# An attention, mixer and expert kernel on one core: the order of all steps read from a table instead of planned, and a third output tile

## The chip, the core and the metric

The kernel runs on one core of one Trainium2 chip. The metric is device microseconds of one execution; less is better. A core has a matrix engine (TensorE, PE in the profile; its weight loads are listed apart as PEld), VectorE (DVE), ScalarE (ACT), GpSimd (POOL), and queues that issue transfers; nearly all of this kernel's transfers are issued by SyncE (SP). Every engine takes its instructions strictly in the order in which the program lists them, and semaphores make one engine wait for another. So an instruction that has to wait holds up everything that stands behind it on its engine.

## The reference

Three layers are computed one after the other for B = 4 sequences of S = 448 tokens with 768 features.

```python
# 1: attention, 12 heads of 64, q and k normalized by their root mean square
q_n, k_n = rmsnorm(q, g_q), rmsnorm(k, g_k)
x = softmax(q_n @ k_n.T / 8) @ v                    # heads side by side: (4, 448, 768)
# 2: mixer: over tokens (448 -> 256 -> 448), then over channels (768 -> 1536 -> 768)
u = x + (relu(x.T @ w_tok1) @ w_tok2).T
x = u + relu(u @ w_ch1) @ w_ch2
# 3: four causal attention "experts" of width 64; each token takes the best two by a gate
logits = x @ w_gate
for e in range(4):
    ye = causal_softmax(x @ wq[e], x @ wk[e]) @ (x @ wv[e]) @ wo[e]
    out += gate(logits, e) * ye
```

All inputs and the output are float32.

## The kernel before

**Stages.** The work is cut by sequence b (0 to 3). For each b there are six pairs of heads of the first attention (`Pair`: `load`, `stack`, `score`, `finish`), the token mixer (`token`), the channel mixer (`channel`), the projections and gate of the experts (`project`), two causal pairs and the output product (`combine`). Pairs are numbered through in tile names, by their keys: k0 to k5 belong to the first sequence, k6 to k11 to the second, k12 and k13 are the first sequence's causal pairs, k14 to k19 belong to the third sequence, and so on. The softmax of one sequence's attention runs beside the channel mixer of the sequence before it, which is nearly pure matrix work.

**Products.** `product` makes a 32-bit product out of three matmuls per block, on operands that were split into a high and a low half (`mm3`, L526; tiles a<-uhl,whl or a<-hid,whl in the profile). `split` makes the two halves: a copy (L437 on ACT, L438 on DVE) and a subtraction (L456, DVE or POOL). The channel weights are split once, stored, and loaded again for later sequences (whl<-kept_c).

**Softmax of a pair.** `weighted` multiplies q by k in row halves of the array (L608), takes the row maxima on DVE (L578), multiplies them by the factors of q's norm (`scale`, L584, DVE or POOL), and takes exponentials on ACT (L593). The weights are then transposed: on the matrix engine for the first nine pairs (`flip`, L632; L656 in causal pairs) or, later, in 32x32 blocks on DVE (`turn`: L706, then sixteen copies per pair, L718, on ACT, DVE or POOL). `attend` multiplies by v in column halves of the array (L731). For the norms, squares are taken on ACT (L876, L886) or POOL (L887) and summed on DVE (L834), and a short chain takes the inverse root (`root`, L843 to L852); from b = 0, pair 2 on, the factors of k are stored to memory (rs<-st, L906), read back spread over partitions (rb<-rs, L971) and multiplied into k (`scaled`: one DVE instruction at L826, or two of POOL at L828 and L829). The channel mixer adds its result into u at L1115 on DVE, the output product leaves through an `ot` tile (L437 or L438) and a store (L1205).

**What sets the order.** No order is written out. `add` records each step with the engines that may do it, an assumed cost on each, what it reads and writes, and how PE's array is split (`mode`: rows, columns or whole). Ring sizes (`RING`) say how many tiles of a name exist; a step that opens a tile waits until the users of the tile that had the place are done. `order` then lays all steps out ten times by priorities (`lay`), with assumed lags between engines (`LAG`), an assumed cost for a change of the array's split (`TURN`) and a clock model, keeps the shortest plan, and `issue` emits the steps in that order, each on the engine that the plan chose.

## Time and profile before

| | us |
|---|---|
| median of 3 runs | 865.03 (862.51 to 867.0) |
| the profiled execution, its own time | 864.52 |
| its span, first to last instruction | 862.6 |
| outside the span | 1.9 |
| PE busy | 818.5 |
| DVE busy | 621.6 |
| ACT busy | 465.4 |
| POOL busy | 159.1 |

The durations below belong to the profiled execution. PE is busy in 95% of the span, but ends of matmuls are modelled, so busy time also holds short waits. The mean granted TensorE clock is 0.994 of full speed.

### The profile page before, as it was taken

The numbers are of one execution on the slowest core, as the hardware profiler recorded it, in microseconds if no ns is written. First come the engines' busy times: TensorE is split into PE (matmuls) and PEld (weight loads), VectorE is DVE, ScalarE is ACT, GpSimd is POOL, SyncE is SP. The second block draws the span as 40 slices with busy tenths as digits, with TensorE's granted clock in tenths as the row PEclk, the third lists the DMA queues.
The fourth block names the chain that finished last, engine by engine and source line by source line (L and its number), as shares of the span: only waits on it lengthen the run. The fifth ranks groups of instructions, "written<-read, shape, count | busy, mean of one in ns | idle before, by whom it ended". The sixth has DMA issues, their size and how long they took to land.

```text
span 862.6 us, 13161 instructions
## 1 busy us (share of the span) xinstructions
PE 818.5 (95%) x4508; PEld 634.1 (74%) x4508; DVE 621.6 (72%) x1290; ACT 465.4 (54%) x1046; POOL 159.1 (18%) x173
## 2 busy tenths in 40 slices
PE   3888889999989999999999998999999999999998
PEld 1445578877765877887676786897776799998787
DVE  6988889999999878826989777933888781114352
ACT  6897765757798546504676554700757631011443
POOL 1243831110463222002132111110130100000000
PEclk9999989999999999999999999999999999999999
DMA  8555678999788927887655514786464406666344
GB/s 235 170 156 150 186 231 267 297 300 298 253 290 229 266 96 224 251 245 212 199 158 157 176 58 135 219 244 214 146 189 132 129 31 217 207 231 203 106 132 168
DMA packets 83202, 168.37 MB, mean 195 GB/s; under 512 B 17504, under 2 KB 39136, under 8 KB 83136
## 3 DMA queue, kind: packets, MB, share of 16 engines
q1 hardware_dynamic: 82992, 167.54, 63.7%
q8 instruction: 36, 0.59, 0.3%
q14 instruction: 30, 0.25, 0.1%
q10 hardware_dynamic: 144, 0.00, 0.0%
HBM read 136.66 MB, written 30.84 MB: 194 GB/s over the span
## 4 chain that ended last, share of the span: by engine, by line
PE 67%; DVE 15%; ACT 6%; DMA 6%; issue 3%; POOL 2%; SPq 1%; ACTq 0%; DVEq 0%; POOLq 0%
PE a L526 49%; PE m L731 8%; PE s L608 7%; ACT s L593 3%; DVE nm L578 3%; DMA w<-in_wc_dram 2%; PE m L757 2%; DVE s L706 1%; DVE s L718 1%; PE s L656 1%; DVE wraw L476 1%; DVE wraw L478 1%; DMA rs<-st 1%; DMA rb<-rs 1%; DVE st L834 1%
## 5 line engine op out<-in xcount | busy, mean ns | idle before, releaser
L526 PE MATMUL a<-uhl,whl 128*128 128x448 f32 x1152 | 246.0, 368 | 3.1 <-ACT ot L437 3.1
L526 PEld LDWEIGHTS a<-uhl,whl 128*128 128x128 f32 x1152 | 215.0, 189 | 35.1 <-issue 10.6
L526 PE MATMUL a<-hid,whl 128*128 128x448 f32 x864 | 181.6, 365 | 2.0 <-DVE u L1115 1.9
L526 PEld LDWEIGHTS a<-hid,whl 128*128 128x128 f32 x864 | 160.3, 188 | 23.7 <-issue 7.0
L593 ACT ACTIVATE s<-s,nm,st 128x448 f32<-128x448 f32 (+1 forms) x192 | 137.0, 723 | 71.7 <-PE m L731 47.1
L608 PE MATMUL s<-k,q 64*128 64x448 f32 (+4 forms) x512 | 111.2, 546 | 9.5 <-ACT s L593 7.4
L578 DVE TENSOR_REDUCE nm<-s 128x2 f32<-128x896 f32 (+1 forms) x96 | 101.1, 1081 | 10.0 <-PE s L608 9.5
L718 ACT COPY s<-s 32x896 f32<-32x896 f32 (+1 forms) x97 | 82.8, 853 | 6.1 <-DVE s L706 4.6
L442 ACT ACTIVATE hid<-a 128x448 fp32r<-128x448 f32 x39 | 21.2, 544 | 119.9 <-PE a L526 119.8
L731 PE MATMUL m<-s,v 128*64 128x448 f32 x384 | 77.5, 545 | 1.7 <-DVE s L718 1.7
L608 PEld LDWEIGHTS s<-k,q 64*112 64x112 f32 (+1 forms) x512 | 40.9, 183 | 49.5 <-issue 22.5
L718 DVE COPY s<-s 32x896 f32<-32x896 f32 (+1 forms) x104 | 71.1, 684 | 1.8
L1115 DVE TENSOR_TENSOR u<-a,u 128x448 f32<-128x448 f32 x48 | 29.8, 620 | 56.5 <-PE a L526 56.2
L706 DVE STREAM_TRANSPOSE s<-s 128x896 f32<-128x896 f32 x60 | 63.4, 1089 | 8.5 <-ACT s L593 6.9
L1104 DVE SCALAR_TENSOR_TENSOR hid<-a,hid 128x448 fp32r<-128x448 f32 x48 | 29.8, 621 | 51.7 <-ACT hid L442 51.1
L731 PEld LDWEIGHTS m<-s,v 128*64 128x64 f32 x384 | 25.8, 136 | 43.5 <-issue 41.3
L456 POOL TENSOR_TENSOR uhl<-u,uhl 128x448 fp32r<-128x448 f32 x27 | 32.3, 1205 | 124.4 <-DVE uhl L438 50.0
L456 POOL TENSOR_TENSOR whl<-wraw,whl 128x384 fp32r<-128x384 f32 (+1 forms) x29 | 32.2, 1117 | 100.1 <-DVE whl L438 44.7
L718 POOL COPY s<-s 32x896 f32<-32x896 f32 (+1 forms) x39 | 34.1, 874 | 80.0 <-DVE s L706 75.9
L593 ACT ACTIVATE s<-s,nm 112x112 f32<-112x112 f32 (+3 forms) x64 | 30.9, 493 | 26.8 <-DVE nm L572 26.3
L526 PE MATMUL a<-whl,uhl 128*112 128x260 f32 x288 | 39.9, 289 | 1.4 <-ACT q L552 1.1
L437 ACT ACTIVATE s<-s 112x448 f32<-112x448 f32 (+5 forms) x52 | 23.9, 501 | 31.0 <-PE s L656 28.5
(145 smaller groups left out, 1077.8 us busy)
## 6 DMA issues: line engine op xcount, KB each, us to landing
whl<-kept_c SPq DMA_DIRECT2D x144, 384.0 KB, 3.7
w<-in_wc_dram SPq DMA_DIRECT2D x48, 384.0 KB, 4.2
kept_c<-whl SPq DMA_DIRECT2D x48, 384.0 KB, 5.4
whl<-kept_qk SPq DMA_DIRECT2D x24, 384.0 KB, 3.6
nat<-in_nat_dram SPq DMA_DIRECT2D x19, 448.0 KB, 4.8
v<-in_vals_dram SPq DMA_DIRECT2D x24, 256.0 KB, 4.1
q<-in_qkt_dram SPq DMA_DIRECT2D x24, 232.0 KB, 4.3
k<-in_qkt_dram SPq DMA_DIRECT2D x22, 224.0 KB, 3.9
```

Source lines behind the costliest of these rows:

```text
L437: lambda e: nc.scalar.activation(dst(), src(), AF.Copy) if e == "ACT"
L442: lambda e: nc.scalar.activation(dst(), src(), AF.Relu) if e == "ACT"
L456: either(n, reads, writes, lambda e: e.tensor_tensor(dst()[:, 1], src(), f(dst()[:, 0]), op=ALU.subtract))
L526: nc.tensor.matmul(acc, lhs[:, x], rhs[:, y], start=first and i == 0, stop=last and i == 2)
L578: lambda e: e.tensor_reduce(nm.t[:R, c], pst.t[:R, :, :w], axis=AX.X, op=ALU.max, negate=True))
L593: lambda j=j: nc.scalar.activation(s.t[:, c, j, :w], pst.t[:R, j, :w], AF.Exp, bias=nm.t[:R, c, j : j + 1], scale=-1.0 if rq is None else ...
L608: nc.tensor.matmul(pst.t[:R, j, :w], q.t[me, CP * c : CP * c + R], k.t[me, :w], start=True, stop=True)
L706: dve(2 * S + 64, [(s, (j, r)) for j in range(2)], [(t, r)], lambda e, r=r: e.transpose(t.t[:, :, 32 * r : 32 * r + 32], s.t[:, r].rearran ...
L718: lambda e, a=a, o=o, w=w, at=at: (nc.scalar.copy if e == "ACT" else ENG[e].tensor_copy)(at(p.t[32 * o : 32 * o + 32, :, P * a : P * a + N ...
L731: nc.tensor.matmul(av.t[64 * j : 64 * j + 64, q0:S], vat(j, c)[1](), p.t[:, j, c, q0:] if causal else p.t[:, 3 * j + c], start=c == 0, sto ...
L1104: lambda e, hl=hl, pa=pa: e.scalar_tensor_tensor(hl.t[:, 1], pa.t[:, :S], 0.0, f(hl.t[:, 0]), op0=ALU.max, op1=ALU.subtract))
L1115: dve(S, [pa], [u], lambda e, u=u, pa=pa: e.tensor_add(u.t, pa.t[:, :S], u.t))
```

## The change

`issue` no longer plans. `read` unpacks a table that is written into the file and holds, for every step, its place in the order and its engine; it was found offline, by annealing the planner's model of the chip under several random delays. The steps and what they depend on are the same, except that `ot` has three tiles instead of two. The assumed costs and lags that the diff also changes are those of the model with which the table was found; when the program is built they set nothing any more.

```diff
@@ RING @@
-    "gt": 2, "g1": 2, "lg": 2, "nm": 4, "sm": 3, "rc": 2, "oT": 8, "xn": 2, "ot": 2,
+    "gt": 2, "g1": 2, "lg": 2, "nm": 4, "sm": 3, "rc": 2, "oT": 8, "xn": 2, "ot": 3,
...
+TABLE = (
...
-    TURN = {None: 0, "rows": 190, "columns": 150}
+    TURN = {None: 0, "rows": 220, "columns": 187}
+    ENTRY = 85
...
+    def read(self):
+
+        n = len(self.steps)
+        raw = zlib.decompress(base64.b85decode(TABLE))
+        lo, hi, by = raw[:n], raw[n : 2 * n], raw[2 * n :]
+        assert len(by) == n
+        out, k, seen = [], 0, set()
+        self.by = [None] * n
+        for a, b, e in zip(lo, hi, by):
+            k = (k + a + 256 * b) % 65536
+            self.by[k] = list(self.LAG)[e]
+            ways, deps = self.steps[k][:2]
+            assert self.by[k] in ways and k not in seen and seen.issuperset(deps)
+            seen.add(k)
+            out.append(k)
+        return out
...
-        for k in self.order():
+        for k in self.read():
             self.steps[k][2](self.by[k])
...
-        return int(2.1 * n + 155)
+        return int(2.2 * n + 155)
...
-            add({"DVE": (130, True), "POOL": (200, True)}, 0, [rq[0]], [(nm, c) for c in cs],
+            add({"DVE": (90, True), "POOL": (200, True)}, 0, [rq[0]], [(nm, c) for c in cs],
...
-                add({"DVE": (dve_ns(S + 60), True), "POOL": (pool_ns(S) + 630, True)}, 0,
+                add({"DVE": (dve_ns(S + 60), True), "POOL": (2700, True)}, 0,
```

All line numbers are 99 higher in the changed kernel (L826 becomes L925, L1115 becomes L1214). PE has the same instructions in another order: the array's split changes 181 times along it, 188 times before. Between the other engines some steps change hands: L584 stands 26 times on POOL (11 before), the copies of L718 96 + 22 times on ACT (75 + 22 before), 63 + 32 on DVE (80 + 24) and 21 + 6 on POOL (25 + 14), where the first number is that of the 32x7x128 form. In the rows below a name such as k17_3298 is the 17th tile of the ring k, and the number behind the underscore only numbers tiles in the program.

ACT at the start of the program before: squares of the first tiles (h10, xhl0, vg0, nat1), the first pair's keys (k0) and its first exponentials (s0).

```order
L876 ACTIVATE s3_145<-h10_117 112x512
L886 ACTIVATE xhl0_118<-xhl0_118 112x1024
L964 ACTIVATE k0_103<-m0_162,gqk_86 128x448
L886 ACTIVATE xhl0_118<-xhl0_118 112x1024
L886 ACTIVATE vg0_106<-vg0_106 112x1024
L886 ACTIVATE nat1_168<-nat1_168 112x1024
L593 ACTIVATE s0_112,sm0_98<-s4_172,nm0_96,st1_140 112x448
```

The same place on ACT in the change.

```order
L975 ACTIVATE s3_139<-h10_117 112x512
L1063 ACTIVATE k0_103<-m0_156,gqk_86 128x448
L985 ACTIVATE xhl0_118<-xhl0_118 112x1024 x2
L985 ACTIVATE nat1_172<-nat1_172 112x1024
L692 ACTIVATE s0_112,sm0_98<-s4_162,nm0_96,st1_136 112x448 x2
L985 ACTIVATE vg0_106<-vg0_106 112x1024
L692 ACTIVATE s0_112,sm0_98<-s5_165,nm0_96,st1_136 112x448
```

The copy of k0 has moved ahead of both squares of xhl0, and the first two exponentials ahead of the square of vg0.

DVE before, in the channel mixer of the second sequence (b = 1): sums into u6 to u10 and, between them, the scaling of the third sequence's keys k17 to k19.

```order
L834 TENSOR_REDUCE st7_2860<-nat15_3877 112x2x8
L1115 TENSOR_TENSOR u6_3290<-a110_3892,u6_3290 128x448
L826 SCALAR_TENSOR_TENSOR k17_3298<-k17_3298,gqk_86,rb13_3940 128x448
L1115 TENSOR_TENSOR u7_3307<-a111_3925,u7_3307 128x448
L826 SCALAR_TENSOR_TENSOR k18_3646<-k18_3646,gqk_86,rb14_3947 128x448
L1115 TENSOR_TENSOR u8_3434<-a112_3949,u8_3434 128x448
L1115 TENSOR_TENSOR u9_3445<-a113_3977,u9_3445 128x448
L826 SCALAR_TENSOR_TENSOR k19_3839<-k19_3839,gqk_86,rb15_3999 128x448
L1115 TENSOR_TENSOR u10_3534<-a114_4005,u10_3534 128x448
```

The same sums on DVE in the change.

```order
L1214 TENSOR_TENSOR u6_3218<-a110_3811,u6_3218 128x448
L1214 TENSOR_TENSOR u7_3258<-a111_3886,u7_3258 128x448
L1214 TENSOR_TENSOR u8_3391<-a112_3911,u8_3391 128x448
L933 TENSOR_REDUCE st7_3857<-nat16_3869 112x2x8
L677 TENSOR_REDUCE nm15_3853<-s86_3974 128x2
L1214 TENSOR_TENSOR u9_3415<-a113_3925,u9_3415 128x448
L777 TENSOR_SCALAR inv6_3991<-sn6_3558 112x8
L1214 TENSOR_TENSOR u10_3519<-a114_3957,u10_3519 128x448
```

The scaling of k17 now stands 13 rows behind the last of these, that of k18 forty rows further, and that of k19 is on POOL; maxima and norm sums of another pair stand between the sums instead.

ACT before, in the channel mixer of the first sequence, where the copies s23<-s22 of pair 10 (k10) stand.

```order
L437 ACTIVATE whl53_2692<-wraw32_2652 128x384
L718 COPY s23_2695<-s22_2645 32x7x128
L718 COPY s23_2695<-s22_2645 32x7x64
L718 COPY s23_2695<-s22_2645 32x7x128 x2
L437 ACTIVATE whl54_2733<-wraw33_2676 128x384
L718 COPY s23_2695<-s22_2645 32x7x128
L593 ACTIVATE s24_2748,sn5_2749<-s60_2682,nm11_2706,st4_375 128x448 x2
L593 ACTIVATE s24_2748,sn5_2749<-s61_2685,nm11_2706,st4_375 128x448 x2
L552 ACTIVATE q12_2778<-a78_2701 128x448
L718 COPY s23_2695<-s22_2645 32x7x64
```

The same copies on ACT in the change.

```order
L536 ACTIVATE whl53_2708<-wraw32_2650 128x384
L817 COPY s23_2718<-s22_2710 32x7x128 x2
L692 ACTIVATE s24_2776,sn5_2777<-s60_2692,nm11_2740,st4_696 128x448 x2
L692 ACTIVATE s24_2776,sn5_2777<-s61_2695,nm11_2740,st4_696 128x448 x2
L536 ACTIVATE whl55_2792<-wraw33_2721 128x384
L817 COPY s23_2718<-s22_2710 32x7x128 x4
```

ACT has six long copies of this pair instead of five long and two short; on DVE there stand three long and three short, six long and one short before. Counted from the first maximum of pair 9 (tile s52) to the first masked maximum of the second causal pair (s72, k13), DVE has 120 rows where it had 130.

## Rows read from the trace of the kernel before

**Rows 1.** The page's busy part: busy us, share of the span, instructions.

```profile
PE 818.5 (95%) x4508; PEld 634.1 (74%) x4508; DVE 621.6 (72%) x1290; ACT 465.4 (54%) x1046; POOL 159.1 (18%) x173
```

**Rows 2.** Busy time by stretch: stretch, its length, engines, clock, DMA, GB/s.

```profile
core 0: us, PE busy (x) PEld busy (x) DVE busy (x) ACT busy (x) POOL busy (x), PEclk, DMA share, GB/s
0.00:130.00 130.00, 103.27 (x572) 62.11 (x573) 109.72 (x216) 98.37 (x233) 50.17 (x60) 0.97 0.63 188
212.00:290.00 78.00, 73.69 (x392) 51.58 (x390) 74.65 (x143) 62.84 (x137) 33.33 (x33) 1.00 0.85 257
540.00:862.00 322.00, 319.08 (x1759) 265.17 (x1757) 171.41 (x391) 122.12 (x277) 20.83 (x22) 1.00 0.56 172
```

**Rows 3.** PE's waits by what ended them: us in total, times, longest.

```profile
PE m L757 <- DVE xn L898: 10.6, 2, 8.8
PE s L608 <- ACT s L593: 7.4, 9, 2.7
PE a L526 <- DVE h L1068: 3.6, 4, 2.7
...
PE a L526 <- ACT ot L437: 3.1, 2, 2.0
PE a L526 <- DVE u L1115: 1.9, 3, 1.5
...
PE a L526 <- DVE lg L1149: 0.3, 1, 0.3
```

**Rows 4.** Timeline of the start: start, us, instruction, idle before it.

```profile
8.77 1.01 PE L757 MATMUL m<-ident,xn 112*128 112x112 f32 x4 [8.77 <-DVE xn L898]
9.32 1.06 ACT L886 ACTIVATE xhl<-xhl 112x1024 f32<-112x1024 f32 x1 [1.92 <-DMA xhl<-in_nat_dram]
10.28 0.62 ACT L964 ACTIVATE k<-m,gqk 128x448 f32<-128x448 f32 x1
10.95 3.33 PE L608 MATMUL s<-k,q 64*112 64x448 f32 x8 [1.17 <-ACT k L964]
14.39 0.16 DVE L584 TENSOR_TENSOR nm<-nm,st 112x2 f32<-112x2 f32 x1
17.02 3.33 PE L608 MATMUL s<-k,q 64*112 64x448 f32 x8 [2.74 <-ACT s L593]
```

**Rows 5.** Busy time of two stretches with a lower granted clock.

```profile
118.00:125.00 7.00, 6.62 (x19) 5.90 (x20) 4.93 (x9) 2.49 (x5) 2.60 (x2) 0.53 0.27 55
336.00:340.00 4.00, 4.00 (x14) 3.57 (x13) 3.83 (x5) 2.70 (x8) 1.34 (x2) 0.57 0.90 299
```

**Rows 6.** Groups of DVE and POOL by form: busy us, mean ns, idle before.

```profile
L718 DVE COPY s<-s 32x896 f32<-32x896 f32 x80 | 59.2, 741 | 1.4
L834 DVE TENSOR_REDUCE st<-nat 112x16 f32<-112x1024 f32 x16 | 19.4, 1211 | 2.4 <-ACT nat L886 2.3
L850 DVE SCALAR_TENSOR_TENSOR st<-st 112x48 f32<-112x48 f32 x18 | 5.4, 298 | 0.6
L584 DVE TENSOR_TENSOR nm<-nm,st 112x2 f32<-112x2 f32 x17 | 5.5, 326 | 0.3
L456 POOL TENSOR_TENSOR uhl<-u,uhl 128x448 fp32r<-128x448 f32 x27 | 32.3, 1205 | 124.4 <-DVE uhl L438 50.0 <-ACT uhl L437 48.6 <-DVE gt L1161 19.7
L584 POOL TENSOR_TENSOR nm<-nm,st 128x4 f32<-128x4 f32 x4 | 0.8, 204 | 68.6 <-DVE nm L578 68.6
```

**Rows 7.** Timeline where the channel mixer of b = 1 starts.

```profile
334.84 0.54 ACT L437 ACTIVATE ot<-a 128x448 f32<-128x448 f32 x1 [0.32 <-DMA out_dram<-ot]
335.44 0.91 PE L526 MATMUL a<-uhl,whl 128*128 128x448 f32 x3 [1.95 <-ACT ot L437]
```

**Rows 8.** Timeline around the sums into u of b = 1.

```profile
372.60 3.87 PE L526 MATMUL a<-hid,whl 128*128 128x448 f32 x18 [0.27 <-DVE u L1115]
376.70 0.68 DVE L826 SCALAR_TENSOR_TENSOR k<-k,gqk,rb 128x448 f32<-128x448 f32 x1 [4.16 <-DMA rb<-rs]
377.31 0.62 DVE L1115 TENSOR_TENSOR u<-a,u 128x448 f32<-128x448 f32 x1
377.97 0.47 PE L526 MATMUL a<-hid,whl 128*128 128x448 f32 x1 [1.50 <-DVE u L1115]
```

**Rows 9.** PE's waits in the pairs beside later channel mixers, from its timeline.

```profile
483.78 3.23 PE L731 MATMUL m<-s,v 128*64 128x448 f32 x16 [1.12 <-DVE s L718]
...
537.04 3.88 PE L526 MATMUL a<-uhl,whl 128*128 128x448 f32 x18 [1.17 <-ACT ot L437]
```

**Rows 10.** PE's timeline around changes of the array's split.

```profile
35.26 1.01 PE L608 MATMUL s<-k,q 64*112 64x448 f32 x4
36.20 0.60 PE L632 MATMUL a<-ident,s 112*128 112x112 f32 x4
...
47.16 1.76 PE L608 MATMUL s<-k,q 64*112 64x448 f32 x8
48.85 0.98 PE L632 MATMUL a<-ident,s 112*128 112x112 f32 x8
```

More of the change, by code (lines that the diff above doesn't have):

```diff
@@ L1 @@
+import base64
 import heapq
+import struct
+import zlib
 from contextlib import ExitStack
@@ L242, in lay @@
                         cost, both = ways[e]
-                cost += (mode != now) * (self.TURN[mode] + self.TURN[now])
+                cost += (mode != now) * (self.TURN[now] if now else self.ENTRY)
             if not back and e in ("DVE", "ACT"):
@@ L395, in pool_ns @@
     def pool_ns(n):
-        return int(2.1 * n + 155)
+        return int(2.2 * n + 155)
     def pass_ns(n):
-        return 0.4531 * n + 0.5
+        return 0.4475 * n + 0.5
     def rows_ns(n):
@@ L404, in flip_ns @@
     def flip_ns(n):
-        return 0.833 * n + 3
+        return 0.695 * n
     ENG = {"DVE": nc.vector, "POOL": nc.gpsimd}
@@ L468, in narrow @@
         load(n, [], [d], lambda: nc.sync.dma_start(d.t[:p, : 2 * n], src.bitcast(U32)))
-        add("ACT", act_ns(n), [(d, 1)], [(r, part)], lambda: nc.scalar.activation(
+        add("ACT", act_ns(n) + 28, [(d, 1)], [(r, part)], lambda: nc.scalar.activation(
             rf(), half(1).bitcast(F32), AF.Copy, scale=2.0 ** -112))
-        add("ACT", act_ns(n), [], [(d, 0)], lambda: nc.scalar.activation(
+        add("ACT", act_ns(n) + 28, [], [(d, 0)], lambda: nc.scalar.activation(
             half(0), half(0), AF.Copy, bias=-0.498, scale=0.999 * 2.0 ** -29))
@@ L571, in veiled @@
             for j in range(2):
-                dve(w, [], [pst, (nm, (c, j))], lambda e, j=j: e.tensor_tensor_reduce(
+                dve(w + 40, [], [pst, (nm, (c, j))], lambda e, j=j: e.tensor_tensor_reduce(
                     pst.t[:CP, j, :w], pst.t[:CP, j, :w], veil[:, S - w :], -1.0, 3e38,
@@ L642, in flip @@
                 heads = sorted({j for m in ms for j in (P * m // S, (P * m + P - 1) // S)})
-                add("PE", flip_ns(CP) * NCH * n, [(s, (j, r)) for j in heads for r in range(NCH)],
+                add("PE", (110 if alone else 88) * NCH * n, [(s, (j, r)) for j in heads for r in range(NCH)],
                     [pt], blocks(ms, at), 0.84)
@@ L658, in mms @@
                             s.t[:CP, r, j, CP * c : CP * c + CP], ident[:CP, :CP])
-            add("PE", flip_ns(CP) * (2 * NCH - 2 * cc - 1),
+            add("PE", 88 * (2 * NCH - 2 * cc - 1) - 10,
                 [(s, (j, r)) for r in range(cc, NCH)], [pst], mms, 0.84)
@@ L705, in turn @@
         for r in range(NCH):
-            dve(2 * S + 64, [(s, (j, r)) for j in range(2)], [(t, r)], lambda e, r=r: e.transpose(
+            dve(2 * S - 4, [(s, (j, r)) for j in range(2)], [(t, r)], lambda e, r=r: e.transpose(
                 t.t[:, :, 32 * r : 32 * r + 32],
@@ L715, in turn @@
                      "DVE": (int(0.583 * n) + 171, True),
-                     **({"POOL": (int(1.1 * n) + 155, True)} if a == o else {})}, 0,
+                     **({"POOL": (int(0.9 * n) + 155, True)} if a == o else {})}, 0,
                     [t], [(p, (a, o))],
@@ L736, in attend @@
         chunks = range(NCH)
-        add("PE", 1860 if causal else 2970,
+        add("PE", 1760 if causal else 2970,
             [p] + [vat(0, c)[0] for c in (chunks if causal else (0,))], [av], mms, 0.9,
@@ L884, in __init__ @@
                 x0 = lambda i=i: x().rearrange("p (t i g) -> p t i g", t=2, i=n)[:, :, i]
-                add({"ACT": (act_ns(1024), False), "POOL": (pool_ns(1024), True)}, 0, [], [(q, part)],
+                add({"ACT": (act_ns(1024), False), "POOL": (1900, True)}, 0, [], [(q, part)],
                     lambda e, qv=qv: nc.scalar.activation(qv(), qv(), AF.Square) if e == "ACT"
@@ L888, in __init__ @@
                 add({"DVE": (dve_ns(1024), False),
-                     "POOL": (sum(pool_ns(16 << k) for k in range(6)), True)}, 0,
+                     "POOL": (3600, True)}, 0,
                     [], [(q, part), (st, i)], lambda e, x0=x0, qv=qv: fold(e, x0(), qv()))
```

75 lines of the change are left out of this document (added).

## Prediction

> **What bounds the kernel now.** I read the page's busy part first: PE works in 95% of the span and DVE in 72% [rows 1], so the matrix engine sets the time and the question is where it stands still. The table by stretch answers that [rows 2]. In the first 130 us PE is idle for 130 - 103.27 = 26.7 us, while DVE works 109.72 and ACT 98.37 of them. From 212 to 290 us, where the second sequence's softmax runs beside the first sequence's channel mixer, PE is idle for 4.3 us, and DVE for only 3.35: there DVE is the bound. From 540 us to the end PE is idle for 2.9 of 322 us: nothing is to be had there. The list of PE's waits gives the same from the other side: its 17 lines add up to 40.3 us, of which 8.8 are the wait for the first transposes [rows 3]. The timeline then shows single waits: at the start [rows 4], where the channel mixer of b = 1 begins [rows 7], between its sums [rows 8], and in the pairs of the third and fourth sequence [rows 9]. After two idle stretches the granted clock fell to its lower level, 1.2 GHz: 7 us show 0.53 of full speed and 4 us show 0.57 [rows 5], so about 7 x 0.47 = 3.3 and 4 x 0.43 = 1.7 us were lost.
>
> So at most 40.3 - 8.8 + 5.0 = 36.5 us could come back without changing PE's own work.
>
> **The change part by part.** The instructions of PE are the same, and by counts and mean durations of the forms the other engines keep their loads too: DVE loses 17 long copies of L718 (17 x 0.741 = 12.6 us [rows 6]) and gets other work in their place. No engine is relieved over the whole; what counts is the place.
>
> *The start.* The copy of k0 began at 10.28, when the first square of xhl0 (9.32 to 10.38) was nearly over, although the transposes that it reads had run from 8.77 to 9.78; the first scores followed at 10.95 [rows 4]. In the change that copy stands ahead of both squares: at least 0.5 us (10.28 - 9.78). The next scores waited 2.74 us, until 17.02, for exponentials that in the change stand before the square of vg0. On DVE the second pair's normalized keys are also made before the first maximum, which meets the second wait for xn in the first line of [rows 3] (10.6 - 8.8 = 1.8). Upper end 1.17 + 2.74 + 1.8 = 5.7. DVE must still sum the same squares before it can go on, so I take 2.0, near the low end.
>
> *The rest of the first 130 us.* 26.7 - 8.77 - 1.17 - 2.74 - 1.8 = 12.2 us of idle PE, in some twenty waits for exponentials and copies [rows 2, 3]. The steps are interleaved in another way throughout, and no single row says what that brings. Bounds 0 and 12.2; DVE and ACT are loaded to 84% and 76%, so most of it can't go: I take a third, 4.1.
>
> *212 to 290 us.* From the first maximum of pair 9 to the first masked one of the second causal pair, DVE has 120 rows for 130. Out go four long copies (4 x 0.741 = 3.0), one sum of squares (1.2) and one norm chain of eleven short instructions (at most 11 x 0.298 = 3.3) [rows 6]; by mean durations other work for some 3.5 us comes in (scaling of one pair's keys, copies of projections), which leaves about 4.0 less. PE can win its 4.3 idle us at most and nothing at least, if the work that was pushed back is late in its turn; it goes to 292 to 320 us and later, where DVE has room. I take 3.0.
>
> *The third output tile.* The last `ot` copy but one began at 334.84, just behind the landing of an earlier store from the same tile, and PE waited 1.95 us for the place in PSUM that it empties [rows 7]; at 537.04 the same wait took 1.17 [rows 9]. A third tile takes the store out of that wait. ACT also had exponentials to do, which stay. Bounds 0 and 3.1; I take 2.6. The low clock from 336 to 340 follows directly on this wait. Bounds 0 and 1.7; I take 1.2. The other low stretch stays in my sum (0, upper end 3.3): the wait before it, for h (2.7 [rows 3]), has much the same products and DVE steps in front of it in the change.
>
> *The keys between the sums.* On DVE the scaling of a key tile waited 4.16 us for a load, the sum into u stood behind it, and PE behind the sum: 0.27 and 1.50 us [rows 8]. In the change the three scalings stand behind the sums or on POOL. On SP the store and the reads of the factors stay between loads of weights, with the store moved behind the weights of the last sums, so that they hold nothing up that these need. Bounds 0 and 1.8; I take 1.8. Next late is the sum itself, which needs only its product.
>
> *The remaining waits*, of 290 to 345 and 470 to 540 us, such as the 1.12 us in [rows 9]: 40.3 - 26.7 - 4.3 - 1.8 - 3.1 = 4.4 us. Bounds 0 and 4.4; half, 2.2.
>
> *Changes of the array's split*, 181 for 188. Four score instructions took 36.20 - 35.26 = 0.94 us with a change before and behind them, eight took 48.85 - 47.16 = 1.69 [rows 10]: four cost 0.75, so two changes cost 0.19. Seven fewer: 0.7 (1.3 if each cost as much as such a pair).
>
> *New waits.* An order laid out on a model of the chip will wait where the model is wrong. No row of before prices that. The nearest is what the planner's own order left: 13.6 us of waits behind the first 130 us. I charge 4.0, a third of it, with 0 and all of the gain as ends.
>
> Sum: 2.0 + 4.1 + 3.0 + 2.6 + 1.2 + 1.8 + 2.2 + 0.7 - 4.0 = 13.6 us. The profiled execution took 864.5 (span 862.6 and 1.9 around it), 0.5 below the median of the three runs; 864.5 - 13.6 = 850.9, so **851**.
>
> **The rivals.** *More is gained.* If two thirds of the 31.5 us of waits behind the first transposes go, and both low-clock stretches, the gain is 21 + 5 = 26: 838. For it speaks that the waits are short and scattered, the kind that a finer order removes, and that modelled ends of matmuls hide further ones in PE's busy time; against it, that DVE is busy for 84% of the first stretch and 96% of the second.
>
> *The change does nothing that counts*: the waits turn up elsewhere, since each engine has the same work. Only the third tile and the moved keys, waits with a cause of their own, then pay, less the new waits: 2.6 + 1.8 - 4.0, about 0 to 2 us: 863. For it speaks that the sum rests on thirds and halves; against it, that the waits of [rows 7, 8] have causes which the change removes.
>
> *Slower: POOL in the chain of the softmax.* L584 lies between the maxima and the exponentials. It moves to POOL 15 times, where it can stand behind a subtraction of 1.205 us [rows 6], and in the change wide scalings do stand right behind such subtractions and behind copies. In the kernel before POOL had idled 68.6 us in all before its four wide ones, and they took 0.204 each [rows 6], so none was held up. To turn the result into a loss of 0.5% (4.3 us), the 15 must lose (13.6 + 4.3) / 15 = 1.2 us each, one full subtraction in front of every one, with nothing for PE to do meanwhile. With 1.5 each it is 22.5 - 13.6 = 8.9 us slower: 873. Against it: beside a channel mixer PE has products to go on with, and only two of POOL's wide scalings are in the stretch that DVE bounds.
>
> One observation belongs here: on DVE, L584 in its 112x2 form took 0.326 us on average [rows 6], but 0.16 us when POOL stood still [rows 4]. The Trainium skill (page "SBUF — State Buffer", section "Who interferes with whom") says that a DVE instruction with two SBUF inputs, or a copy in a two-port mode, and a POOL instruction that reads SBUF exclude each other for their whole length. The longer mean agrees with such a lock, without showing it. By that rule each scaling moved to POOL could start a whole DVE copy late, 0.741 us, together 11.1 us, and the sum would be 862 instead of 851 if all of it lay on the path.
>
> **How the numbers follow.** The forecast, 842 to 858 around 851, has a chance of 0.60; more gained (838) 0.20; no change that counts (863) 0.12; slower (873) 0.08. Half a per cent, 4.3 us, is about what a measurement of this kernel can tell from no change. The first two cases are faster by more, the third lies within: faster 0.80, same 0.12, slower 0.08. The range that leaves out no more than two in ten runs from 836 to 864; all upper ends together would reach 864.5 - 37.8 = 827, which I leave out, as I do the slower case.
>
> **What would show it.** At the start, the first scores below 10.4 us after the span's start. No wait of PE for `ot` above 0.5 us, and no low-clock stretch where the channel mixer of b = 1 begins. No wait of PE for a sum of u behind a key's scaling. Between pair 9 and the second causal pair, PE idle below 2 us. PE's waits in total near 24 us instead of 40.3, with those of the first 130 us near 20. The prediction is wrong if the waits keep their sum under other names, if the list of waits shows exponentials waiting for POOL's L683, or if the first stretch alone becomes shorter by more than 10 us.

## The result, and the profile after

| | before | after |
|---|---|---|
| median, us | 864.41 (862.51 to 867.0, 4 runs) | 840.25 (838.88 to 841.59, 4 runs) |
| the profiled execution, its own time | 864.52 | 838.88 |
| its span | 862.6 | 837.1 |

The ratio is 0.972, 95% interval 0.970 to 0.974: 24 us faster, where the forecast said 13.6 (851). The wide range, 836 to 864, holds it; the forecast's own range, 842 to 858, just missed it, and the first rival, "more is gained" with 838, came nearest.

The page's busy part, which answers to [rows 1]:

```profile
PE 810.9 (97%) x4508; PEld 630.6 (75%) x4508; DVE 614.6 (73%) x1292; ACT 465.9 (56%) x1033; POOL 154.8 (18%) x181
```

The other engines keep their busy time to within 3%; PE's share rose because the span shrank. The table by stretch, with columns as in [rows 2]:

```profile
0.00:130.00 130.00, 112.48 (x651) 71.41 (x652) 117.28 (x239) 110.00 (x257) 36.21 (x55) 1.00 0.76 220
212.00:290.00 78.00, 76.29 (x450) 55.82 (x450) 69.72 (x164) 58.70 (x134) 28.35 (x30) 1.00 0.78 240
540.00:837.00 297.00, 293.17 (x1636) 244.48 (x1635) 162.55 (x368) 104.75 (x234) 18.22 (x19) 1.00 0.56 171
```

In the first 130 us PE is idle for 17.5 us instead of 26.7, DVE works 117.28 instead of 109.72 and ACT 110.00 instead of 98.37, and the clock is whole: the work was drawn forward. From 212 to 290 us PE's idle time fell from 4.3 to 1.7 us. PE's list of waits, which answers to [rows 3], has 15 lines that add up to 22.0 us (40.3 before); the first lines and two further ones are

```profile
PE m L856 <- DVE xn L997: 8.1, 1, 8.1
PE s L707 <- ACT s L692: 3.9, 4, 1.6
PE a L731 <- ACT s L536: 1.3, 5, 0.4
...
PE a L625 <- DVE ot L537: 0.7, 1, 0.7
...
PE a L625 <- DVE h L1167: 0.3, 1, 0.3
```

Of the lines of before, the waits for h (3.6), for `ot` (3.1) and for the last sums of u (1.9) are gone or small. The stretches around the first products of two channel mixers, which had the low clock in [rows 5], with columns as above:

```profile
112.00:120.00 8.00, 8.00 (x42) 7.50 (x41) 7.75 (x14) 5.76 (x11) 2.32 (x2) 1.00 0.66 218
316.00:322.00 6.00, 6.00 (x32) 5.63 (x31) 5.18 (x7) 4.60 (x11) 4.09 (x4) 1.00 0.91 296
```

**Where the time came from.** Both kernels issue the same 4508 matmuls, so the two traces can be compared at equal work: each matmul counts with the shortest pace that its form shows, the counts are summed in the order of each trace, and the *lead* is how much earlier a kernel has done what the profiled execution of before had done at a given time. The same measure is used for every experiment below. These values are worked out from the starts of all matmuls of one execution each. They scatter: before, ring, rest, rest2, norm and keys have the same beginning, yet lie between -1.5 and 2.5 at 44 us, and at 143 us before, ring, rest2 and keys, still in the same order, lie between -1.9 and 4.2. So a value is good to some 3 us.

```
lead (us) when before is at   44     94    143    204    248    293    341    383    465    530    end
full change                  1.7    5.4   12.9   12.7   14.3   15.7   20.4   22.7   22.4   25.0   25.5
ring                        -1.5   -2.0   -1.0   -1.0    0.6   -0.1    2.0    1.7    1.9    2.0    2.3
first                       -0.2    3.5    8.7    8.4   10.0    9.9   11.7   11.9   11.3   11.5   11.2
rest                         0.2   -1.9   -9.3   -9.5   -7.8   -6.5   -1.8    0.5    0.7    3.3    3.9
rest2                        2.5    0.6    4.2    4.2   -2.4   -1.1    3.6    6.0    6.1    8.4    8.9
keysdve                      0.5    1.2    2.5    2.5    3.8    3.6    5.4    6.3    6.5    6.5    6.8
norm                        -1.3   -2.0   -1.4   -1.4   -1.9   -1.3   -2.1   -2.5   -2.3   -2.2   -1.8
keys                        -0.9   -2.9   -1.9   -1.9   -1.6   -2.0   -1.5    0.6   -3.4   -3.3   -4.1
ot2                          1.4    5.1   12.5   12.4   14.0   15.3   16.6   16.4   16.6   18.9   11.0
```

Of 25.5 us, 11.2 come between 44 and 143 us, 3.0 between 204 and 293, 4.7 to 341, 2.3 to 383, 2.6 between 465 and 530, and about nothing after that. The lists agree: 18.3 us of listed waits (40.3 to 22.0) and the 5.0 us that before lost to the low clock make 23.3.

### The profile page after: what moved, and what is told of

Its sections match the earlier page's. It is cut to its first block, busy times and chain, and to the rows that moved or that the text cites. A ratio compares the mean times of both kernels' runs of the same rounds, so it can differ in the third digit from the quotient of the medians.

```text
span 837.1 us, 13116 instructions
## 1 busy us (share of the span) xinstructions
PE 810.9 (97%) x4508; PEld 630.6 (75%) x4508; DVE 614.6 (73%) x1292; ACT 465.9 (56%) x1033; POOL 154.8 (18%) x181
## 4 chain that ended last, share of the span: by engine, by line
PE 82%; DVE 12%; ACT 3%; issue 2%; DMA 1%; POOL 0%; SPq 0%; ACTq 0%; DVEq 0%
PE a L625 58%; PE s L707 9%; PE m L830 9%; PE m L856 2%; DVE nm L677 2%; DVE s L805 2%; PE s L755 2%; PE a L731 1%; DVE s L817 1%; ACT s L692 1%; PE s L731 1%; DVE wraw L575 1%; DVE wraw L577 1%; DMA h<-in_nat_dram 1%; DMA kept_c<-whl 0%
## 5 line engine op out<-in xcount | busy, mean ns | idle before, releaser
L625 PE MATMUL a<-uhl,whl 128*128 128x448 f32 x1152 | 242.9, 365 | 0.9 <-DVE hid L1203 0.9
L817 ACT COPY s<-s 32x896 f32<-32x896 f32 (+1 forms) x118 | 102.5, 868 | 28.1 <-DVE s L805 18.4
L1214 DVE TENSOR_TENSOR u<-a,u 128x448 f32<-128x448 f32 x48 | 29.8, 621 | 58.0 <-PE a L625 57.7
L555 POOL TENSOR_TENSOR uhl<-u,uhl 128x448 fp32r<-128x448 f32 x31 | 35.9, 1172 | 175.7 <-DVE uhl L537 115.6
L692 ACT ACTIVATE s<-s,nm 112x336 f32<-112x336 f32 (+3 forms) x64 | 31.1, 492 | 63.0 <-DVE nm L671 61.7
L817 DVE COPY s<-s 32x896 f32<-32x896 f32 (+1 forms) x95 | 61.3, 645 | 2.3
L541 ACT ACTIVATE hid<-a 128x448 fp32r<-128x448 f32 x28 | 15.2, 544 | 76.2 <-PE a L625 76.2
L692 ACT ACTIVATION_READ_ACCUMULATOR s<-s,nm,st 128x1 f32 (+1 forms) x192 | 38.3, 199 | 0.0
```

Of the source, the lines that this page charges most:

```text
L555: either(n, reads, writes, lambda e: e.tensor_tensor(dst()[:, 1], src(), f(dst()[:, 0]), op=ALU.subtract))
L625: nc.tensor.matmul(acc, lhs[:, x], rhs[:, y], start=first and i == 0, stop=last and i == 2)
L692: lambda j=j: nc.scalar.activation(s.t[:, c, j, :w], pst.t[:R, j, :w], AF.Exp, bias=nm.t[:R, c, j : j + 1], scale=-1.0 if rq is None else ...
L817: lambda e, a=a, o=o, w=w, at=at: (nc.scalar.copy if e == "ACT" else ENG[e].tensor_copy)(at(p.t[32 * o : 32 * o + 32, :, P * a : P * a + N ...
L1214: dve(S, [pa], [u], lambda e, u=u, pa=pa: e.tensor_add(u.t, pa.t[:, :S], u.t))
```

## The experiments

The theory was that the gain is many short waits of PE taken out by a finer interleaving, and that stretches add up. The rivals were the third tile, the corrected costs, the choice of engines, and a few single steps that sat in the wrong place. Every ratio is to the kernel before, in runs on the same chip.

**ring: only the third tile.** The table holds the planner's own order and engines.

```diff
-    order and engines: the change's
+    order and engines: the planner's, as in the kernel before
     "ot": 3
```

> The planner's order and engines of the kernel before, written into the table, with three ot tiles: the third tile alone. Theory (each gain has its place and keeps it): the third tile takes 1.95 us of waiting where the channel mixer of b = 1 begins and 1.17 us at b = 2 away, perhaps with 1.7 us of low clock: 860 to 862 us against 864.4. Rival (ACT's exponentials stand ahead of the copy, so the tile is worth nothing by itself): 864 to 865.

Measured: 862.96 us, ratio 0.999 (0.997 to 1.001). The time lies between the two expectations; the wait at the copies is as the rival had it, 1.52 of the 1.95 us of [rows 7] stayed. From PE's timeline, then from ACT's:

```profile
334.98 7.48 PE L625 MATMUL a<-uhl,whl 128*128 128x448 f32 x36 [1.52 <-ACT ot L536]
```

```profile
333.68 0.72 ACT L692 ACTIVATE s<-s,nm,st 128x448 f32<-128x448 f32 x1 [3.03 <-DVE nm L683]
...
334.39 0.53 ACT L536 ACTIVATE ot<-a 128x448 f32<-128x448 f32 x1
```

In [rows 7] the landing of the store ended only 0.32 us of ACT's idle time; for the rest, by this run, ACT comes late to the copy anyway, behind an exponential that waited 3.03 us for its scaled maxima. The wait is 1.91 to 2.02 us in the three traces that have the planner's order here and two tiles (before, norm, keys), and 1.52 in the three with three tiles (ring, keysdve, normkeys). So in this order the tile takes some 0.4 us, too little to be told in the time. The six copies lie 11 us apart here, in the view of the tile `ot` (first and last start at the end):

```profile
L536 ACT ACTIVATE ot<-a x4: 532/552/565, 325.5 to 334.4; 128x448 f32<-128x448 f32 x4
L537 DVE COPY ot<-a x2: 585/605/625, 326.7 to 336.7; 128x448 f32<-128x448 f32 x2
```

**replan: only the corrected costs.** The planner plans with the new costs; no table, three tiles.

```diff
-        for k in self.read():
+        for k in self.order():
```

> The planner runs again, with the changed assumed costs and three ot tiles, and no table: what the corrected costs bring without a search. Theory (the search over orders is what pays): within 6 us of the kernel before, 858 to 870. Rival (the corrected costs are what pays, and the table only freezes a plan that the planner would nearly find itself): 840 to 848.

Measured: 866.54 us, ratio 1.006 (1.003 to 1.009): a little slower. The corrected costs by themselves are not the gain; the table is.

**first and rest: one half of the order each.** The cut lies before the first product of the first channel mixer.

```diff
+    first: the change's first 602 steps, then the planner's order of what is left
+    rest:  the planner's first 572 steps, then the change's order of what is left
```

> The first 602 of 3840 steps of the table, up to the first product of the channel mixer of b = 0, and then all other steps in the planner's order and on its engines. Theory (the gain of the first stretch is its own and is kept): by equal PE work the table was 12.9 us ahead at 143 us, 3.3 of it a low clock that did not occur, so 850 to 855. Rival (time won early is given back, because the later order then waits for transfers or for DVE): 860 or more.

> The first 572 of 3840 steps in the planner's order and on its engines, up to the first product of the channel mixer of b = 0, then all other steps in the table's order. Theory (additive): 864.4 less the 12.7 us that the table gained behind 143 us: 850 to 854; with the experiment on the first part the two losses against 840 add up to 24. Rival (the table's later order only works behind its own beginning): 858 or more.

Measured: first 852.87 us, 0.990 (0.986 to 0.994); rest 861.28, 0.998 (0.995 to 1.001). The first stretch keeps its gain by itself (11.2 of lead at the end), as the theory had it. By its time the rest wins nothing, as the rival had it, but the lead shows a loss at the seam, at 115 to 143 us, and a gain of 13.4 behind it (-9.5 at 204 us to 3.9). PE's timeline has the loss: transposes of a pair whose exponentials the other beginning had not got ready.

```profile
130.08 0.82 PE L731 MATMUL s<-ident,s 112*128 112x112 f32 x3 [5.48 <-ACT s L692]
```

**rest2: the rest again, from a better cut,** where only six steps of either order lie on the other side.

```diff
+    the planner's first 1080 steps (to some 211 us), then the change's order of what is left
```

> The first 1080 steps (to about 211 us) in the planner's order and engines, all later ones by the table. At this cut only six steps stand on the other side of it in one order than in the other (at the earlier cut before the channel products it was 24), so the seam should cost little. My theory: what the table gains from 212 us on adds to whatever stands ahead of it, and the 9.5 us that the first such splice lost lay at its seam. Lead of the full change over the kernel before: 12.7 us at 204 us, 25.5 at the end, so this one should keep 12.8: about 851 us, ratio 0.985, and its lead should be near 0 at 210 us, 3 at 290, 8 at 345, 12 at the end. Rival: the later order pays only because its own beginning had left the engines ahead with their work; then 3 to 4 us stay as in the first splice (about 860, ratio 0.996).

Measured: 859.47 us, 0.993 (0.991 to 0.996), near the rival's 860 and not the theory's 851; the profiled execution, 855.48, is its fastest. It loses 6.6 us of lead between 204 and 248 us, again at one wait close behind the cut:

```profile
223.20 3.73 PE L625 MATMUL a<-hid,whl 128*128 128x448 f32 x9 [7.22 <-DVE u L1214]
```

From 248 us on it gains 11.3 us (-2.4 to 8.9); the full change gains 11.2 there (14.3 to 25.5). So in these two traces the later order pays behind the seam whatever stood ahead: stretches add up, as far as one execution of each can tell, and my estimate of the seam (nearly nothing) was wrong. What the table wins from 212 to 248 us stays untested.

**eng and ord: order without engines, engines without order.** 406 steps have another engine in the table.

```diff
+    eng: the change's order, each step on the planner's engine
+    ord: the planner's order, each step on the change's engine
```

> The order of the table, but every step on the engine that the planner gave it (406 of the steps go back). Theory that the order of the steps is the gain: most of it stays, at least 17 of the 25 us (ratio 0.973 to 0.980). Rival, that the choice of engine is the gain (the planner's beginning keeps GpSimd busy for 17.0 of the 20 us from 80 to 100, the table for 7.6): at least half goes, ratio 0.986 or more. A third way, that order and engines only pay together: the ratio is over 1.0.

> The planner's order, but every step on the engine that the table gives it. Order alone is the gain: nothing is won, ratio 0.998 to 1.01. Engines alone: ratio 0.986 or less. Both only together: over 1.0. With the run of the table's order on the planner's engines this gives the two shares; if they add up, the two ratios together make 0.972.

Measured: eng 898.26 us, 1.039 (1.037 to 1.042); ord 906.01, 1.047 (1.045 to 1.050). Neither half is a gain: each alone costs more than both together bring. The longest of PE's waits, first in eng, then in ord:

```profile
PE s L707 <- ACT s L692: 15.0, 12, 4.3
PE a L625 <- DVE hid L1203: 11.4, 6, 4.4
```

```profile
PE s L707 <- ACT s L692: 24.0, 23, 4.0
```

That fits queues in which a step on another engine stands at the wrong place: the scores wait for exponentials for 15 and 24 us, where before had 7.4 [rows 3] and the change 3.9.

**keysdve: six steps change engine.** From 80 to 100 us POOL was busy for 16.15 us in ring and 7.64 in the full change; the table has scalings of keys on DVE that the planner gave to POOL.

```diff
     order: the planner's, "ot": 3
-    scaling of k4 to k9 on POOL (two instructions each)
+    scaling of k4 to k9 on DVE (one instruction each)
```

> The planner's order and engines with three output tiles, and one edit: the scalings of the keys k4 to k9 (six steps, each a product with gqk and one with rb, about 2.9 us together on GpSimd, as in the table) go from GpSimd to VectorE. Theory: the stretch from 80 to 125 us lost 7 us more than the table's because GpSimd was full there (keys, then halves of split weights late by some 5 us, then products that wait for h and u); with the keys away the halves come earlier and the low clock at 118 us goes with the 2.7 us wait ahead of it: 4 to 8 us faster, ratio 0.991 to 0.995. Rival: VectorE is busy 84 to 93% there, and six scalings put 3 to 4 us on it ahead of maxima and h: the wait moves there, ratio 0.998 to 1.004. Against the ring run (0.9991) either is told apart.

Measured: 860.43 us, 0.995 (0.993 to 0.997): some 4 us, against ring's nothing, the low end of what the theory gave. But not in the way expected. The windows of ring and then of keysdve, and a row of PE's timeline in keysdve:

```profile
80.00:100.00 20.00, 15.68 (x97) 9.01 (x96) 16.75 (x23) 14.51 (x33) 16.15 (x17) 1.00 0.52 155
```

```profile
80.00:100.00 20.00, 15.68 (x101) 9.19 (x100) 16.77 (x28) 15.31 (x36) 9.76 (x12) 1.00 0.50 157
...
117.15 4.26 PE L625 MATMUL a<-t,h 128*128 128x448 f32 x12 [2.72 <-DVE h L1167]
```

POOL lost 6.4 us of work there, PE's busy time stayed the same, and the wait for h stands unchanged. The lead grows a little at a time (0.5, 1.2, 2.5), and by 143 us it is only 2.5.

**norm: the chain ahead of h.** In the planner's order DVE works on a chain of eleven norm instructions from 113.5 to 117.9 us, and the evictions into h for which PE waited 2.72 us stand behind it.

```diff
-L942 TENSOR_SCALAR st_375<-st_375 112x48
-... (ten more)
 L1167 SCALAR_TENSOR_TENSOR h_1238<-a_1212,h_1238 128x256
 L1167 SCALAR_TENSOR_TENSOR h_1238<-a_1234,h_1238 128x256
...
 L1185 TENSOR_TENSOR u_1266<-a_1285,u_1266 128x448
+L942 TENSOR_SCALAR st_375<-st_375 112x48
+... (ten more)
```

> The kernel before (planner's order and engines, two output tiles) with one edit: the norm chain of 48 columns that VectorE works on from 113.5 to 117.9 us (4.4 us, one step of eleven instructions) and the store behind it go behind the two evictions into h and the last two sums into u of this stretch; the table has the chain 108 places later. Theory: TensorE's wait of 2.72 us for h at 118.4 was the chain's, and the low clock from 118 to 125 us (3.3 us) followed from the idle time ahead of it: 2.5 to 6 us faster, ratio 0.993 to 0.997. Rival: what the chain feeds (the factors of the next pair's keys) or the halves of u are as late, and the wait moves: ratio 0.999 to 1.003.

Measured: 864.44 us, 1.000 (0.998 to 1.003). The wait for h is gone and another of the same length stands 8 us later, for halves of u behind the same chain, with the low clock behind it. Rows of PE's timeline and a window, then rows of DVE's timeline:

```profile
117.90 2.66 PE L625 MATMUL a<-t,h 128*128 128x448 f32 x12
...
126.80 3.48 PE L625 MATMUL a<-uhl,whl 128*128 128x448 f32 x9 [2.82 <-DVE uhl L555]
...
126.80:130.00 3.20, 3.20 (x9) 2.88 (x10) 3.17 (x9) 2.50 (x9) 0.00 (x0) 0.55 0.71 166
```

```profile
121.60 0.61 DVE L942 TENSOR_SCALAR st<-st 112x48 f32<-112x48 f32 x1
...
126.12 0.62 DVE L555 TENSOR_TENSOR uhl<-u,uhl 128x448 fp32r<-128x448 f32 x1
```

So the rival holds: the wait moves. But it moved with the chain, which stands ahead of both waits. The table has the chain's step 108 places later, where PE has a long run of channel products and does not wait; rows of DVE's timeline, then of PE's, in the change:

```profile
123.12 0.18 DVE L942 TENSOR_SCALAR st<-st 112x48 f32<-112x48 f32 x1
```

```profile
109.01 2.68 PE L625 MATMUL a<-t,h 128*128 128x448 f32 x12
111.53 10.97 PE L625 MATMUL a<-uhl,whl 128*128 128x448 f32 x54
```

Whether the chain alone, put that far back, would free PE was not run; norm does not rule it out.

**normkeys: both edits,** with three tiles.

```diff
+    norm's two steps moved, and k4 to k9 scaled on DVE
```

> The last edit and the scalings of the keys k4 to k9 from GpSimd to VectorE together, with three output tiles. If the two remove different waits they add up: keys alone gave 0.995, so 0.988 to 0.992 in all (855 to 858 us), and most of the 11 us that the table wins in the first 145 us is explained by two steps' place and engine. Rival: both only remove the same low clock, or VectorE is now too full: 0.994 or more.

Measured: 860.58 us, 0.995 (0.992 to 0.997), what keysdve gives alone. The two do not add up, and together they are some 4 of the 11 us; PE waits 2.44 us for uhl at 124.83. This pair of steps does not explain the first stretch.

**keys: the forecast's term by itself,** with two tiles. Rows of DVE:

```diff
 L1214 TENSOR_TENSOR u_3290<-a_3892,u_3290 128x448
-L925 SCALAR_TENSOR_TENSOR k_3298<-k_3298,gqk,rb_3940 128x448
 L1214 TENSOR_TENSOR u_3307<-a_3925,u_3307 128x448
...
 L1214 TENSOR_TENSOR u_3549<-a_4028,u_3549 128x448
+L925 SCALAR_TENSOR_TENSOR k_3298<-k_3298,gqk,rb_3940 128x448
+L925 SCALAR_TENSOR_TENSOR k_3646<-k_3646,gqk,rb_3947 128x448
+L925 SCALAR_TENSOR_TENSOR k_3839<-k_3839,gqk,rb_4075 128x448
 L933 TENSOR_REDUCE st_2860<-nat_4048 112x2x8
```

> The kernel before with one edit: the scalings of the keys k17, k18 and k19 stand behind the two last sums into u of the channel mixer, not between them, with the load that needs the first of them. My forecast's term: 1.8 us less (waits of 0.27 and 1.50 us), ratio 0.998, near what can be told; in the trace no wait of TensorE for u between 336 and 390 us. Rival: the scores of these pairs then wait for their keys, and nothing is won: ratio 1.000 or more, with a wait of the scores between 390 and 470 us.

Measured: 865.48 us, 1.000 (0.998 to 1.003). PE no longer waits for u between 336 and 390 us, and between 341 and 383 us the lead grows by 2.1, near the forecast's 1.8 though within the scatter; by 465 us 4.0 are lost again. The third scaling still waits for its load, and what stands behind it now is the eviction into hid. Rows of DVE's timeline, of PE's, and the window behind the wait:

```profile
392.56 0.69 DVE L925 SCALAR_TENSOR_TENSOR k<-k,gqk,rb 128x448 f32<-128x448 f32 x1 [3.47 <-DMA rb<-rs]
...
394.30 0.61 DVE L1203 SCALAR_TENSOR_TENSOR hid<-a,hid 128x448 fp32r<-128x448 f32 x1
```

```profile
394.96 4.88 PE L625 MATMUL a<-uhl,whl 128*128 128x448 f32 x15 [2.32 <-DVE hid L1203]
...
395.00:399.00 4.00, 4.00 (x12) 3.57 (x13) 0.62 (x1) 0.76 (x2) 0.00 (x0) 0.57 0.90 238
```

I had expected 1.8 us less, or a later wait of the scores and nothing won. Nothing was won, but it was the products that waited. The table has the third scaling on POOL, where nothing stands behind it that PE needs soon.

**ot2: the full change with two output tiles.** Where a copy would need a tile that is not free, it and what depends on it stand some places later (16 steps move).

```diff
-    "ot": 3
+    "ot": 2
```

> The full change with two output tiles instead of three; where a step needs a tile that is not yet free it stands a few places later. Forecast's term: the third tile is worth 2.6 us and the low clock behind its wait 1.2, so up to 3.8 us slower than the full change (ratio 0.972 to 0.977 to the kernel before). Rival, from the ring run (0.9991, with 1.5 us of the wait left): the wait went because the table has two of the six copies into these tiles some 30 us later, not because of the tile; then 0.971 to 0.973, and no wait over 1 us at these copies.

Measured: 853.83 us, 0.987 (0.985 to 0.990), some 13 us slower than the full change by the two ratios, far more than either theory gave. Its lead is that of the full change to 293 us, 3.8 less at 341, 6.3 less at 383 and 14.5 less at the end. A row of DVE and the next wait of PE at the second of the two places, then the window behind it:

```profile
514.99 0.62 DVE L537 COPY ot<-a 128x448 f32<-128x448 f32 x1 [2.18 <-DMA out_dram<-ot]
```

```profile
515.67 0.88 PE L625 MATMUL a<-xhl,w 128*128 128x448 f32 x3 [1.92 <-DVE ot L537]
...
529.52 6.65 PE L625 MATMUL a<-uhl,whl 128*128 128x448 f32 x20 [4.75 <-DVE hid L1203]
...
529.50:535.00 5.50, 5.48 (x15) 4.91 (x16) 1.31 (x2) 1.81 (x3) 0.00 (x0) 0.53 0.81 256
```

With two tiles a copy waits for a landing (2.18 us here, 4.32 at 329.09, 3.35 at 533.54), the place in PSUM that it empties stays full, and PE's products behind it go later. PE's two longest waits behind the start, 4.75 us and 2.84 at 323.71, are for hid, though, each with the low clock behind it (0.53 for 5.5 us, 0.50 for 5.3): how much of the 13 us the waiting copies cost, and how much the moved steps, these rows do not show. The full change packs the six copies of the first place into 8 us; in its view of `ot`:

```profile
L536 ACT ACTIVATE ot<-a x3: 544/545/545, 309.3 to 315.8; 128x448 f32<-128x448 f32 x3
L537 DVE COPY ot<-a x3: 585/625/625, 309.9 to 317.1; 128x448 f32<-128x448 f32 x3
```

So the rival had it the wrong way round: the copies are not spread out, they are packed, where with two tiles the last one starts at 329.09. Ring's order, spread over 11 us, had no use for the tile. The order was adapted for two tiles, not searched again, so 13 us is what this order loses when it is fitted to two tiles, not what two tiles cost at best.

## Why the prediction was right, and where its size was off

**The bound** was right: the gain is PE's idle time and the low clock, nearly all of it before 540 us. Of the 31.5 us of waits behind the first transposes 17.6 went (13.9 are left), and all 5.0 of the low clock, close to what the first rival assumed. The two terms that were far off, the first 130 us and the new waits, both erred to the same side, so the hit in the wide range owes nothing to errors that cancel.

**The rest of the first 130 us (4.1)** is the term that was mis-sized. With the low clock, which I had left at 0, it measured 11.2 instead of 4.1: 3.3 for the clock and some 7.9 of the 12.2 us of waits, two thirds and not a third. By PE's idle time it is much the same: over 523 matmuls each, from 44 to 143 us in before and from 42.3 to 130.1 in the change, it fell from 10.4 to 3.1. The 3.3 are not the order's alone: with the same order and the same wait, rest2 lost nothing there and ring half as much (see the last section). "DVE and ACT are loaded to 84% and 76%, so most of it can't go" was the false step: they went to 90% and 85%, with more work drawn into the stretch. The wait for h at its end had "much the same products and DVE steps in front of it" one by one, but was gone: there the norm chain stands behind the channel mixer's first products. By norm, a shorter move of that chain only moves the wait. My sentence on what would make the prediction wrong named this case (the first stretch alone shorter by more than 10 us).

**New waits (-4.0)** did not come: the waits have the sum 22.0, against 24 forecast. An order searched under random delays had no wait above 1.6 us behind the first one. eng and ord show what new waits can cost where order and engines were not searched together: 33 and 41 us.

**212 to 290 us (3.0)** was right: 3.0 of lead, 2.6 of PE's idle time.

**The start (2.0)**: the first scores came at 9.84 (10.95 in [rows 4]) and the next at 15.50, as PE's timeline has it.

```profile
8.11 1.00 PE L856 MATMUL m<-ident,xn 112*128 112x112 f32 x4 [8.11 <-DVE xn L997]
9.84 3.33 PE L707 MATMUL s<-k,q 64*112 64x448 f32 x8 [0.73 <-ACT k L1063]
...
15.50 1.84 PE L707 MATMUL s<-k,q 64*112 64x448 f32 x4 [1.39 <-ACT s L692]
```

Of these 1.11 us only 0.45 come behind the transposes, where the copy of k0 stands ahead of the squares (1.73 us from the first transpose to the first scores, 2.18 before); the other 0.66 are an earlier start of the transposes (8.11, 8.77 before), ahead of which DVE makes xn before a sum of squares and not behind it. That start also varies: with the planner's beginning it lies between 8.22 (rest2) and 9.23 (norm), and the first scores come at 10.22 in rest2 and 10.35 in keysdve. So my sign, first scores below 10.4, could not tell the orders apart. The lead at 44 us is 1.7, -0.2 and 1.4 in the three traces with this beginning and between -1.5 and 2.5 in the six with the planner's (mean -0.2), so about 1, no better known than this scatter.

**The third tile (2.6) and the low clock behind it (1.2)**: the waits went (3.1 to 0.7 for `ot`, still above the 0.5 of my sign; the clock 1.00), and the lead grew by 4.7 up to 341 us. But the reason I gave, the store that is taken out of the wait, is worth some 0.4 us of it alone (ring) and up to 13 us in the table's order (ot2): I priced the tile by the wait that before showed. Nor does the low clock hang on the tile alone: in keys, with two tiles and a wait of 2.02 us here, it stayed at 1.00.

**The keys between the sums (1.8)**: 2.3 of lead to 383 us and no such wait in the list, but by itself the edit only moves the wait (keys). **The remaining waits (2.2)**: 2.6 between 465 and 530 us, and a part of the 4.7. The split changes (0.7) can't be told apart in this.

**The rivals.** The exponentials do wait for POOL's L683, as the slower rival had it; ACT's list of waits says so:

```profile
ACT s L692 <- POOL nm L683: 22.7, 11, 9.3
```

Yet PE's wait for exponentials fell from 7.4 to 3.9: POOL itself mostly waited for the maxima, so this sign was badly chosen. The prices that I gave a moved scaling, 1.2 us behind a subtraction and 0.741 behind a DVE copy, did not come: POOL was idle ahead of 23 of the 26, and they took 0.26 us on average, the longest 0.79. Two of their groups in the change:

```profile
L683 POOL TENSOR_TENSOR nm<-nm,st 128x4 f32<-128x4 f32 x14 | 3.8, 269 | 117.7 <-DVE nm L677 110.4 <-DVE oT L849 7.1
L683 POOL TENSOR_TENSOR nm<-nm,st 112x2 f32<-112x2 f32 x10 | 2.6, 264 | 40.2 <-DVE nm L677 40.1 <-DVE nm L683 0.2
```

The other direction I overlooked. The Trainium skill (page "SBUF — State Buffer", section "Who interferes with whom") states that a DVE instruction with two SBUF inputs, or in a two-port mode, and a GpSimd instruction that reads SBUF shut each other out, and that the first to issue blocks the other. The mean of DVE's long copies hides it (731 ns in the change, 741 in [rows 6]), but single rows of before agree. The 326 ns that I took from [rows 6] are fourteen instructions of about 0.16 us and three of 0.38, 0.88 and 2.07, each of which ends with a POOL instruction. One of these, then the norm chain ahead of h, in before:

```profile
78.81 2.38 POOL L456 TENSOR_TENSOR xhl<-xn,xhl 112x1024 fp32r<-112x1024 f32 x1 [2.42 <-ACT xhl L437]
79.14 2.07 DVE L584 TENSOR_TENSOR nm<-nm,st 112x2 f32<-112x2 f32 x1
```

```profile
113.73 2.25 POOL L456 TENSOR_TENSOR uhl<-u,uhl 128x448 fp32r<-128x448 f32 x2 [0.54 <-ACT uhl L437]
113.74 1.19 DVE L847 TENSOR_SCALAR st<-st 112x48 int32<-112x48 int32 x1
114.97 1.08 DVE L850 SCALAR_TENSOR_TENSOR st<-st 112x48 f32<-112x48 f32 x1
```

In the change the same two instructions of the chain take 0.19 and 0.21 us. Counting what DVE's instructions took above the median of their form over all traces, where that is over 0.1 us, the first 130 us lost 9.6 us of DVE in before (13 instructions) and 5.0 in the change (5); ring lost 11.5 and keysdve 6.9.

**Open** is what makes up some 7 of the 11 us of the first stretch: six scalings moved from POOL bring some 4, the norm chain moved behind the last sums nothing, up to 3.3 are a low clock that does not come in every execution, and no other part was taken alone. A candidate is the 4.6 us less that DVE loses beside POOL; that PE's waits fell by it is argued, not shown. Open is also whether the norm chain at its place in the table would bring more.

## What to carry to other kernels

Order and choice of engine, where they were searched together, are one decision: here each alone cost 4 to 5%, both together gained 2.8%, and a later part of the searched order lost some 7 us at the seam to another beginning, twice, before it paid. What one more buffer is worth depends on the order: nothing that could be told with the old one, some 13 us against a two-tile version of the one that was searched with it; price it there, not by the wait that it takes away. A wait behind an overloaded engine can move when one row moves, as in norm and keys; ask what the engine has to do before the place, over the whole stretch. Look at single rows before you trust a mean: three instructions of seventeen hid the price of POOL's neighbourhood in one. And take the scatter of a measure from kernels with the same order before you read a stretch by it.

## What I had not expected of the hardware

A wait of PE beside channel products often costs half to three quarters more than its length, since the granted clock falls behind it to its lower level (1.2 instead of 2.4 GHz). After 2.82 us it was 0.55 for 3.2 us (norm), after 2.32 us 0.57 for 4.0 us (keys), after 4.75 us 0.53 for 5.5 us (ot2): 1.4, 1.7 and 2.6 us more. It is not certain: after 2.44 us in normkeys and 1.52 in ring the clock stayed at 1.00, while in the kernel before 1.95 us were followed by 0.57 [rows 5, 7].

The same order even has it both ways. In before, ring and rest2 PE runs the same steps up to 211 us and waits for h at the same place: 2.72 us in before, with 0.53 for 7 us behind it [rows 5], 2.70 in rest2 and 2.52 in ring. PE's timeline and the window in rest2, then the window in ring:

```profile
116.51 2.68 PE L625 MATMUL a<-t,h 128*128 128x448 f32 x12 [2.70 <-DVE h L1167]
...
118.00:125.00 7.00, 7.00 (x36) 6.55 (x36) 6.80 (x15) 6.14 (x14) 2.84 (x3) 1.00 0.48 134
```

```profile
118.00:125.00 7.00, 4.52 (x15) 4.09 (x16) 5.31 (x15) 2.85 (x7) 1.07 (x2) 0.76 0.39 116
```

So before's 3.3 us at this place were 0 in rest2 and about half (7 x 0.24 = 1.7) in ring: neither the order nor the length of the wait decides it.
